# Second MLP layer, second token chunk: seven quarter products in place of sixteen plain units, for batches 2 to 7

## The chip, the cores and the metric

The kernel runs on one core of one Trainium2 chip. The time is the device time in microseconds (us) of one execution. TensorE is called PE below, VectorE DVE, ScalarE ACT, GpSimd POOL and the engine that issues the DMAs SP, as in the profile.

## The reference, cut to what matters

```python
# q, k, v: (8 batches, 8 heads, 576 tokens, 64), float32; w_ch1: (512, 2048); w_ch2: (2048, 512)
scores = q @ k.T / 8                              # per batch and head
scores = where(scores >= 32nd largest of its row, scores, -1e9)
x = (softmax(scores) @ v) -> (8, 576, 512)        # heads side by side
u = x + real(fft(fft(x, axis=1), axis=2))
un = (u - mean(u)) / sqrt(var(u) + 1e-6)          # over the 512 channels
out = u + relu(un @ w_ch1) @ w_ch2                # float32, (8, 576, 512)
```

## The kernel before

Batches are counted from 0 in the code (`b`); "batches 2 to 7" of the title are `b` = 1 to 6.

**One loop over attention tiles sets the order.** `items` holds 288 tiles of 128 query rows and one head (36 in a batch). Each turn of the last loop is a step: it issues, by hand and in a fixed order, the scores of a tile to come (PE, line 360, copied out by ACT in line 363), the search for the 32 largest values of a tile (DVE, lines 381 and 383: four `max`, three `match_replace`), the mask (ACT, line 397, then a subtraction on POOL, line 400), the exponential (ACT, line 406), the transposes (PE, line 427, copied out by ACT in line 430) and, at the end of a head pair, the product with v (PE, line 464). Every engine runs what it is given strictly in that order, and waits where an operand is not there.

**The rest of a batch is fitted into these steps.** When the four head pairs of batch b are done, its Fourier transform follows while the tiles of batch b+1 run: folded sums on POOL (lines 549, 565, 602), two pairs of transforms over the tokens (`dft_tokens`, line 634, PSUM tiles `yp_{b}_{par}_0` and `_1`; ACT copies each of them out with three instructions, lines 658 to 660), then the transforms over the channels (`dft_channels`, line 682, tiles `mp`; ACT copies `us` out, line 699; POOL adds them, line 705), the transposes of the normalised rows (line 747, tiles `tpu`), and then the MLP as a queue of units.

**The MLP units.** `mlp_units(b)` makes a list: for chunk 0 (tokens in tiles 0, 1 and the 64 rows of tile 4: 320 columns) and chunk 1 (tiles 2 and 3: 256 columns) 16 units `hidden` (four matmuls each, line 832, ReLU by ACT in line 836 into `hT`), and then the second layer. `one_unit` takes the next of the queue; `level` spreads the queue over the steps up to the next batch's arrival, so that PE gets about the same planned time in each step. `dft_tokens` first takes all `hidden` units that are still in the queue.

**The second layer in its two forms.** The plain form, `back` (line 859), has for each tile of 128 tokens 8 units of two matmuls of 512 columns; the sum stays in one PSUM bank, is scaled by ACT into a buffer (line 886; `hT`'s spare end for tile 2) and added to x by POOL (line 888), and for tile 3 it is scaled and added by DVE in one instruction (line 874). The form in seven products, `fast` (line 1029 for all its matmuls), takes the two tiles and the two halves of the hidden dimension as a 2 by 2 matrix of quarters and does with 7 products of quarters what takes 8: 14 units `p2 p1 p5 p4 p6 p3 p7`, each in two parts, of four matmuls of 256 columns. For that

- POOL forms sums of quarters of `hT` in place (`mix`, line 974, four of them in two parts each: quarters "21", "11", "12", "22"),
- SP brings sums of quarters of `w2`, kept in DRAM, into the places of two quarters of `w2` (`bring`, line 775: T1 and T2 into `w2_12`, T4 and T3 into `w2_21`, then the originals B12 and B21 again),
- five results go through ACT (line 999, into `room(n)`) and POOL (line 1001) into x, and two by DVE (line 987).

`later` puts POOL's part on a list `sums`, from which `some_sums` takes what fits into a step; `need` forces an entry out just before the PE instruction that depends on it. Two PSUM tiles are held through the seven products: `cv` (p2, p5, p3) and `cw` (p1, p4, p6, p7).

**The three banks.** `hidden`, `back`, `fast`, `yp`, `mp` and `tpu` (for all but the last batch, whose `yp`, `mp` and `tpu` have other banks) share three PSUM banks, handed out by `bank`: it takes the first of the list `banks_free` and, unless the tile is held, puts it at the end again at once. A held tile takes its bank off the list until it is freed.

In the kernel before, the seven products are used for chunk 0 of every batch but the first, and for both chunks of the last batch; chunk 1 of `b` = 1 to 6 and all of `b` = 0 use `back`.

Of the kernel before, what the change touches and what calls it, by code (L numbers as in the profile page):

```python
# [64 lines left out]
def kernel(  # L65
# [20 lines left out]
    NIT = DF // P  # L86
# [7 lines left out]
    CW = (2 * P + TAIL, 2 * P)  # L94
# [26 lines left out]
    def bank(shape, name, hold=False):  # L121
        n = banks_free.pop(0)
        t = ps_m.tile(shape, F32, name=name, tag=f"m{n}", bufs=1)
        if not hold:
            banks_free.append(n)
            return t
        return t, lambda: banks_free.append(n)
# [638 lines left out]
    DH = DM // 2  # L766
# [5 lines left out]
    def bring(o, place, part):  # L772
        kcs = slice(NK // 2 * part, NK // 2 * (part + 1))
        dst = place[part] if isinstance(place, list) else place[:, kcs]
        nc.sync.dma_start(out=dst, in_=scr[:, o, kcs, :])
# [19 lines left out]
    sums, summed = [], set()  # L795
# [8 lines left out]
    def need(key):  # L804
        if key in summed:
            return

        kind = next(s[3] for s in sums if s[0] == key)
        for s in [s for s in sums if s[3] == kind]:
            sums.remove(s)  # L810
            s[2]()
            summed.add(s[0])
            if s[0] == key:
                break
# [3 lines left out]
    def mlp_units(b):  # L818
        x = x_of[b]
        last = b == B - 1  # L820
        hTs, hT_of = {}, {}

        def hidden(ch, it):
            w, unT = CW[ch], unT_of[b, ch]
            if ch not in hTs:
                hTs[ch] = batp.tile([P, NIT, CW[0]], F32, name=f"hT_{b}_{ch}", tag="hT")
                hT_of[ch] = hTs[ch].rearrange("p i c -> p (i c)")[:, 0:NIT * w].rearrange(
                    "p (i c) -> p i c", c=w
                )
            hp = bank([P, CW[0]], f"hp_{b}_{ch}_{it}")  # L830
            for dt in range(NDT):
                nc.tensor.matmul(  # L832
                    hp[:, 0:w], lhsT=w1[:, dt, P * it:P * (it + 1)], rhs=unT[:, dt, 0:w],
                    start=(dt == 0), stop=(dt == NDT - 1),
                )
            nc.scalar.activation(out=hT_of[ch][:, it, :], in_=hp[:, 0:w], func=AF.Relu)  # L836
# [10 lines left out]
        def ct_tile():  # L847
            if not cts:
                cts.append(batp.tile([P, 3, DM], F32, name=f"ct_{b}", tag="fold_s"))
            return cts[0]  # L850
# [83 lines left out]
        def fast(ch):  # L934
# [22 lines left out]
                }  # L957

            def room(n):
                return ct_tile().rearrange("p t c -> p (t c)")[:, DH * n:DH * (n + 1)]  # L960

            def later(key, us, fn, soon=False):

                n = sum(s[3] for s in sums) if soon else len(sums)
                sums.insert(n, ((b, ch, *key), us, fn, soon))
                if last:
                    need((b, ch, *key))
# [12 lines left out]
            def to_x(t, cols, src, n, then=lambda: None):  # L980


                xt = x[:, t, cols].rearrange("p (e c) -> p e c", c=DH)
                e = xt.shape[1]
                if n is None or last:
                    def add():
                        nc.vector.scalar_tensor_tensor(
                            out=xt,
                            in0=src.rearrange("p (e c) -> p e c", e=1).to_broadcast([P, e, DH]),
                            scalar=rs[:, t:t + 1], in1=xt, op0=ALU.mult, op1=ALU.add,  # L990
                        )
                        then()
                    if last:
                        add()
                    else:
                        late_next.append(add)
                    return
                r = room(n)
                nc.scalar.mul(out=r, in_=src, mul=rs[:, t:t + 1])
                xt = x[:, t, cols]  # L1000
                later(("x", n), 0.75, lambda: nc.gpsimd.tensor_tensor(
                    out=xt, in0=xt, in1=r, op=ALU.add
                ))
# [20 lines left out]
            def product(name, cols, a, rhs_of, part, start):  # L1024


                dst = half_bank(name, cols)
                for kc in range(NK // 2 * part, NK // 2 * (part + 1)):
                    nc.tensor.matmul(  # L1029
                        dst, lhsT=h()[a][:, kc, :], rhs=rhs_of(kc), start=start and kc == 0,  # L1030
                        stop=kc == NK - 1, skip_group_check=True,
                    )
                return dst
# [10 lines left out]
            def p2(part):  # L1044
                c = product("v", lo, "12", lambda kc: w2_21[:, kc], part, True)
                if not last:
                    bring(T4, second, part)
                if part:
                    to_x(ta, lo, c, 0)

            def p1(part):
                c = product("w", lo, "11", b11, part, True)
                if part:
                    to_x(ta, lo, c, 1)
                    mix("11", "21", "11")
                    mix("12", "12", "11")

            def p5(part):
                need((b, ch, "21", part))
                c = product("v", hi, "21", first, part, False)  # L1060
                bring(T2, w2_12, part)
                if part:
                    to_x(tb, hi, c, 2)
# [9 lines left out]
            def p6(part):  # L1073
                need((b, ch, "11", part))
                c = product("w", lo, "11", first, part, False)
                if ch == 0:
                    bring(B12, w2_12, part)
                if part:
                    to_x(ta, hi, c, 4)
# [15 lines left out]
            def begin():  # L1095
# [7 lines left out]
            ] + [  # L1103
                (1.75, lambda f=f, part=part: f(part), "back")
                for f in (p2, p1, p5, p4, p6, p3, p7) for part in range(2)
            ]

        units = []
        for ch in range(2):
            units += [  # L1110
                (8 * CW[ch] / 1200.0, lambda ch=ch, it=it: hidden(ch, it), "hidden")
                for it in range(NIT)
            ]
            seven = b and ch == 0 or last
            if seven:
                begin, products = fast(ch)
                units.insert(1 - NIT, begin)
                units += products
            for t in [t for t in CHUNKS[ch] if t == 4 or not seven]:
                units += [  # L1120
                    (1.75, lambda ch=ch, t=t, p=p: back(ch, t, p), "back")
                    for p in range(4 if t == 4 else 8)
                ]
# [120 lines left out]
    for b in range(B):  # L1244
        end = PER_BATCH * (b + 1) - 1
        last = b == B - 1
# [45 lines left out]
        for n, t in enumerate((0, 1, 4, 2, 3)):  # L1292
            quick = first or last
            s = fc + (0 if first else n // 3 if last else n // 2)
# [7 lines left out]
        at(s + 1, "begin" if quick else "dve", lambda b=b: rsqrt(b))  # L1302
        arrivals.append(s + (1 if quick else 2))
        at(arrivals[-1], "units", lambda b=b: (queue if b else waiting).extend(mlp_units(b)))

    queue, waiting, pending, written, now, out_next = [], [], [], set(), [0], []
# [40 lines left out]
    i, carry = 0, 0.0  # L1347
# [157 lines left out]
```

## Time and profile before

| what | value |
|---|---|
| time, median of 4 runs (lowest, highest) | 1911.6 us (1910.61, 1913.67) |
| time of the profiled execution | 1910.46 us |
| its span, first to last instruction | 1908.7 us |
| mean granted PE clock | 0.974 |
| busy: PE, weight loads, DVE, ACT, POOL | 94%, 62%, 83%, 63%, 46% of the span |
| matmuls of the plain form, `cp` L859 | 512 records, 240.6 us busy |
| matmuls of the seven products, `cw` and `cv` L1029 in `w` | 448 and 384 records, 106.8 and 90.7 us busy |
| `mix` on POOL, L974 | 64, mean 1276 ns |
| DMA queue 1 | 109.33 MB, 20.2% of 16 engines |
| the chain that ended last | PE 79%, DVE 9%, ACT 6% |

How to read it: a float32 matmul of the program shows as two records, so two matmuls of 512 columns are "x4" in the timeline, and four of 256 columns "x8". The mean duration of a matmul overlaps with the next; what one costs is the distance from its start to the start of what follows. "Idle before" names what the engine waited for.

### The profile page before, as it was taken

The page shows a single profiled execution, that of the slowest core. Times are in us where ns is not written, and L with a number is a line of the kernel's source. Part 1 is how long each engine was busy: PE and PEld are TensorE (multiplying, and loading weights), DVE is VectorE, ACT ScalarE, POOL GpSimd, SP SyncE. Part 2 cuts the span into 40 slices and gives each one's busy share as a digit, 9 for nine tenths or more (in the row PEclk, how much of TensorE's full clock was granted, in tenths as well). Part 3 has the DMA queues.
Part 4 walks back from the last instruction along what each step waited for, and adds up shares of the span by engine and source line. Part 5 has one row for each costly group of instructions (what it writes and reads, how often), then busy time and mean ns, then how long its engine had stood idle before and what let it go on. Part 6 is the DMA issues. An engine that isn't in the chain of part 4 may idle for free.

```text
span 1908.7 us, 28279 instructions
## 1 busy us (share of the span) xinstructions
PE 1799.8 (94%) x9008; PEld 1192.5 (62%) x9008; DVE 1582.0 (83%) x3277; ACT 1210.3 (63%) x3078; POOL 876.5 (46%) x1158
## 2 busy tenths in 40 slices
PE   6567799999999999999999999999999999999999
PEld 3344465474666756766567656667567656667677
DVE  7999989999999999989898998888899898862110
ACT  6878657676766767666666667666676667652100
POOL 4768543545534454345535454345535454341012
PEclk7778899999999999999999999999999999999999
DMA  5323002211114111140014101140013102030132
GB/s 168 112 85 108 20 13 63 86 56 25 47 24 120 31 26 41 45 118 19 22 44 114 43 15 50 42 121 19 19 47 101 52 17 59 23 103 6 50 106 74
DMA packets 184340, 111.34 MB, mean 58 GB/s; under 512 B 125953, under 2 KB 174209, under 8 KB 184193
## 3 DMA queue, kind: packets, MB, share of 16 engines
q1 hardware_dynamic: 183408, 109.33, 20.2%
q8 instruction: 72, 1.18, 0.3%
q14 instruction: 76, 0.61, 0.1%
q10 hardware_dynamic: 784, 0.21, 0.1%
HBM read 93.76 MB, written 15.73 MB: 57 GB/s over the span
## 4 chain that ended last, share of the span: by engine, by line
PE 79%; DVE 9%; ACT 6%; POOL 2%; DMA 2%; issue 2%; SPq 0%; POOLq 0%; DVEq 0%; ACTq 0%
PE hp L832 25%; PE cp L859 11%; PE o L464 7%; PE tpP L427 6%; PE sp L360 6%; PE cw L1029 5%; PE cv L1029 4%; DVE m L381 4%; PE mp L682 3%; PE yp L634 3%; DVE wk L383 3%; PE cp L898 3%; PE sp_t L330 2%; ACT wk L406 1%; POOL wk L400 1%
## 5 line engine op out<-in xcount | busy, mean ns | idle before, releaser
L400 POOL TENSOR_TENSOR wk<-S,wk 128x576 f32<-128x576 f32 x288 | 408.5, 1418 | 775.0 <-ACT wk L397 745.9
L381 DVE MAX8 m<-wk 128x8 f32<-128x576 f32 x864 | 626.3, 749 | 6.1
L832 PE MATMUL hp<-unT,w 128*128 128x256 f32 (+1 forms) x2048 | 538.2, 409 | 2.6 <-ACT unT L750 2.6
L832 PEld LDWEIGHTS hp<-unT,w 128*128 128x128 f32 x2048 | 373.6, 191 | 124.1 <-issue 24.8
L383 DVE MATCH_REPLACE8 wk<-m,wk 128x576 f32<-128x576 f32 x576 | 427.5, 742 | 0.0
L406 ACT ACTIVATE wk<-wk,nt 128x576 f32<-128x576 f32 x288 | 224.8, 781 | 70.1 <-POOL wk L400 66.0
L427 PE MATMUL tpP<-ident,wk 128*128 128x128 f32 x1152 | 183.2, 283 | 67.5 <-ACT wk L406 43.7
L430 ACT COPY PT<-tpP 128x512 f32<-128x512 f32 (+1 forms) x320 | 171.3, 546 | 111.2 <-PE tpP L427 108.9
L859 PE MATMUL cp<-w,hT 128*128 128x512 f32 x512 | 240.6, 598 | 0.0
L397 ACT ACTIVATE wk<-S,nt 128x576 f32<-128x576 f32 x288 | 226.9, 788 | 17.2 <-POOL nt L390 16.0
L427 PEld LDWEIGHTS tpP<-ident,wk 128*128 128x128 f32 x1152 | 140.7, 145 | 141.3 <-ACT wk L406 64.8
L836 ACT ACTIVATE hT<-hp 128x320 f32<-128x320 f32 (+1 forms) x256 | 104.9, 410 | 193.8 <-PE hp L832 191.7
L381 DVE MAX8 m<-S 128x8 f32<-128x576 f32 x288 | 213.7, 742 | 5.3 <-ACT S L334 5.3
L383 DVE MATCH_REPLACE8 wk<-m,S 128x576 f32<-128x576 f32 x288 | 213.6, 742 | 0.0
L464 PE MATMUL o<-PT,v 128*64 128x256 f32 (+3 forms) x1440 | 193.3, 411 | 2.0 <-ACT PT L430 1.9
L363 ACT COPY S<-sp 128x512 f32<-128x512 f32 (+1 forms) x264 | 141.9, 589 | 54.1 <-PE sp L360 53.9
L360 PE MATMUL sp<-kT,qT 64*128 64x512 f32 (+1 forms) x528 | 161.2, 669 | 4.2 <-ACT means L1217 3.3
L464 PEld LDWEIGHTS o<-PT,v 128*64 128x64 f32 x1440 | 110.7, 151 | 72.8 <-issue 15.7
L859 PEld LDWEIGHTS cp<-w,hT 128*128 128x128 f32 x512 | 88.8, 190 | 86.3 <-issue 86.2
L974 POOL TENSOR_TENSOR hT<-hT 128x512 f32<-128x512 f32 x64 | 81.5, 1276 | 100.8 <-ACT hT L836 89.1
L1029 PE MATMUL cw<-w,hT 128*128 128x256 f32 x448 | 106.8, 383 | 2.3 <-POOL nt L390 1.2
L1029 PEld LDWEIGHTS cw<-w,hT 128*128 128x128 f32 x448 | 81.4, 190 | 20.0 <-issue 5.2
(143 smaller groups left out, 2149.0 us busy)
## 6 DMA issues: line engine op xcount, KB each, us to landing
w<-w_parts SPq DMA_DIRECT2D x82, 512.0 KB, 4.4
space<-in_moe_w_ch_dram SPq DMA_DIRECT2D x32, 512.0 KB, 3.5
nat<-in_q_dram SPq DMA_DIRECT2D x128, 64.0 KB, 2.1
v<-in_v_dram SPq DMA_DIRECT2D x128, 64.0 KB, 2.1
out_dram<-x SPq DMA_DIRECT2D x32, 256.0 KB, 2.1
nat<-in_k_dram SPq DMA_DIRECT2D x124, 64.0 KB, 2.1
w_parts<-w_t SPq DMA_DIRECT2D x8, 512.0 KB, 2.9
w_s<-w_parts SPq DMA_DIRECT2D x8, 512.0 KB, 5.0
```

Of the source, the lines that this page charges most:

```text
L360: nc.tensor.matmul(sp[r], lhsT=qT[hd, q_cols], rhs=kT[hd, :], start=True, stop=True)
L381: ops.append(lambda src=src, m8=m8: nc.vector.max(out=m8, in_=src))
L383: ops.append(lambda src=src, m8=m8: nc.vector.match_replace(w, m8, src, NEG))
L397: nc.scalar.activation(out=w, in_=Ssb[i], func=AF.Relu, scale=-FAR, bias=Nt[i][:, 1:2])
L400: nc.gpsimd.tensor_tensor(out=w, in0=Ssb.pop(i), in1=w, op=ALU.subtract)
L406: nc.scalar.activation(out=w, in_=w, func=AF.Exp, bias=Nt.pop(i)[:, 0:1], accum_out=den_t[pair % 3][:, c:c + 1],)
L427: nc.tensor.transpose(tp[:, c, :], p_sb[:, k0 + P * c:k0 + P * (c + 1)], ident)
L430: nc.scalar.copy(out=pt[:, NF * he:NF * (he + 1), col:col + w], in_=tp[:, :, o:o + w])
L464: nc.tensor.matmul(o[D * e:D * (e + 1), c0:c1], lhsT=vv[:, c, e, :], rhs=pt[:, 2 * NF if c == NF else NF * e + c, c0:c1], start=(c == 0), ...
L832: nc.tensor.matmul(hp[:, 0:w], lhsT=w1[:, dt, P * it:P * (it + 1)], rhs=unT[:, dt, 0:w], start=(dt == 0), stop=(dt == NDT - 1),)
L859: nc.tensor.matmul(cp, lhsT=hT[:, it, P * n:P * (n + 1)], rhs=w2[:, it, :], start=(it == 0), stop=(it == NIT - 1),)
L1029: nc.tensor.matmul(dst, lhsT=h()[a][:, kc, :], rhs=rhs_of(kc), start=start and kc == 0, stop=kc == NK - 1, skip_group_check=True,)
```

## The change

Chunk 1 of batches `b` = 1 to 6 is put through `fast` as well (`seven = b > 0`). The results of its five scaled products go into the four places of 256 columns that `hT`'s buffer has left over behind chunk 1's 16 x 256 columns; the fifth takes the first place again, after its POOL addition has been issued. Where a new `hT` tile is begun, all entries that are still on the list `sums` are issued first. B12 is brought back after p6 in these chunks too.

```diff
         def hidden(ch, it):
             w, unT = CW[ch], unT_of[b, ch]
             if ch not in hTs:
+                for s in list(sums):
+                    need(s[0])
                 hTs[ch] = batp.tile([P, NIT, CW[0]], F32, name=f"hT_{b}_{ch}", tag="hT")
...
             def room(n):
+                if ch:
+                    n0 = NIT * CW[1] + DH * (n % 4)
+                    return hTs[1].rearrange("p i c -> p (i c)")[:, n0:n0 + DH]
                 return ct_tile().rearrange("p t c -> p (t c)")[:, DH * n:DH * (n + 1)]
...
+                if ch and n == 4:
+                    need((b, ch, "x", 0))
                 r = room(n)
                 nc.scalar.mul(out=r, in_=src, mul=rs[:, t:t + 1])
...
                 c = product("w", lo, "11", first, part, False)
-                if ch == 0:
+                if not (last and ch):
                     bring(B12, w2_12, part)
...
-            seven = b and ch == 0 or last
+            seven = b > 0
```

## Prediction

> **What bounds the kernel now.** I read the busy times by window first. A middle batch lasts 216.23 us, from one batch's first token transform to the next one's:
>
> ```profile
> core 0: us, PE busy (x) PEld busy (x) DVE busy (x) ACT busy (x) POOL busy (x), PEclk, DMA share, GB/s
> 891.89:1108.12 216.23, 215.08 (x1106) 142.87 (x1105) 192.22 (x398) 145.11 (x372) 99.16 (x137) 1.00 0.19 52
> ```
>
> PE has 1.15 us without work, DVE 24, POOL 117, and the clock is full. So in a middle batch, what PE is spared shortens the kernel, and what PE waits lengthens it. The PE timeline gives the price of a unit in both forms:
>
> ```profile
> 1022.52 1.89 PE L1029 MATMUL cw<-w,hT 128*128 128x256 f32 x8
> 1024.25 0.38 PE L504 MATMUL tpx<-ident,xT 128*128 128x128 f32 x2
> ...
> 1112.93 1.88 PE L859 MATMUL cp<-w,hT 128*128 128x512 f32 x4
> 1114.65 0.71 PE L274 MATMUL tpq<-ident,nat 128*128 128x128 f32 x5
> ```
>
> From start to next start, a unit of the seven products takes 1.73 us and a plain unit 1.72 us.
>
> **What it spares.** Chunk 1 has 16 plain units (27.5 us) and gets 14 (24.2 us): 3.3 us in each of six batches, **19.8 us**. In the order that the changed program issues, one unit less stands before the first token transform and one less after the second; thirteen stand between the two transforms in both. The weights are loaded 112 times instead of 64, 190 ns each; these loads run beside the matmuls, and the 1.73 us above already holds eight of them (1.52 us), so they cost nothing. Were they not hidden, 48 more would cost 9.1 us a batch. The Trainium skill ("Perfetto Trace Analysis", Identifying the Most-Contended Engine) wants TensorE judged by the busy share of the weight loads, not of the matmuls; by that the change would load the engine more, 55 us in all, and the row above decides against it.
>
> **What it costs: banks.** Two held tiles leave one of the three banks. In the order of bank uses before, no tile follows another at once in the same bank. In the changed program it happens at ten places where PE can go on only after ACT has copied the first tile out (a further six have other work between, or wait for the same copies anyway). The rows from before, with two banks to take turns, for PE and then ACT:
>
> ```profile
> 1147.30 0.41 PE L634 MATMUL yp<-fs,ftail 128*1 128x145 f32 x2
> 1147.65 0.76 PE L634 MATMUL yp<-fs,fg 128*128 128x145 f32 x4
> ...
> 1150.93 3.72 PE L682 MATMUL mp<-fd,y 128*128 128x256 f32 x16
> ```
>
> ```profile
> 1147.75 0.42 ACT L658 COPY y<-yp 128x288 f32<-128x288 f32 x1 [2.80 <-PE yp L634]
> 1148.06 0.30 ACT L659 COPY y<-yp 128x144 f32<-128x144 f32 x1
> 1148.22 0.41 ACT L660 ACTIVATE y<-yp,sg 128x144 f32<-128x144 f32 x1
> ...
> 1153.69 0.65 ACT L699 COPY us<-mp 128x512 f32<-128x512 f32 x1
> ```
>
> The second `yp` began at 1147.65, while ACT was still to copy the first until 1148.63. In one bank it begins 0.1 us after that: 1.1 us later. This is so in both pairs of b = 1 and in the second pair of b = 2 to 5: six times, **6.5 us**. In b = 2 and 5 p3 ends just before the second transform, so its bank is still held at the channel transforms, and the first two `mp` share one: the second would begin at 1152.65 (half of the group of 3.72), but the copy of the first ends at 1154.34, as ACT has masks and scores in front of it: 1.8 us, twice, **3.6 us**. At the start of the last batch the second `hp` waits for one ReLU (436 ns and the hand-over): **0.6 us**. The skill says it as a rule ("Perfetto Trace Analysis", Matmuls): "Independent matmul groups should rotate through different PSUM banks so the ACT/DVE evacuation of one overlaps the next group's matmuls". It sets no price; without these stalls the sum would be 10.7 us lower.
>
> **What it costs: POOL's sums.** Eight `mix` of 1276 ns and five additions of 730 ns replace one addition of 1272 ns: 12.6 us more POOL work a batch, now beside the folds. POOL has 117 us free, so the amount is hidden. What counts is the place in its queue. In this stretch the folds take what a step leaves for sums, so half of the mixes are forced out by `need`, behind that step's mask (L400). The rows of chunk 0 show how long that is, PE, ACT and POOL in turn:
>
> ```profile
> 1028.56 1.13 PE L360 MATMUL sp<-kT,qT 64*128 64x512 f32 x4
> 1029.62 1.99 PE L1029 MATMUL cw<-w,hT 128*128 128x256 f32 x8
> ...
> 1033.62 0.38 PE L330 MATMUL sp_t<-kt,qT 128*128 128x128 f32 x2
> 1034.39 1.97 PE L1029 MATMUL cw<-w,hT 128*128 128x256 f32 x8 [0.39 <-POOL nt L390]
> ```
>
> ```profile
> 1033.82 0.47 ACT L999 ACTIVATE ct<-cw,gi 128x256 f32<-128x256 f32 x1
> ```
>
> ```profile
> 1031.60 1.41 POOL L400 TENSOR_TENSOR wk<-S,wk 128x576 f32<-128x576 f32 x1 [3.79 <-ACT wk L397]
> 1032.97 1.28 POOL L974 TENSOR_TENSOR hT<-hT 128x512 f32<-128x512 f32 x1
> ```
>
> The scores of the step end at 1029.62; copies and the mask's ACT half follow, the mask starts at 1031.60 and the mix behind it ends at 1034.25: with the hand-over, 4.7 us after the scores. In the changed order PE reaches a product that needs such a mix after 2.16 us in b = 1 (p7) and b = 4 (p3; one unit and a transpose after the scores), after 3.9 in b = 3, and after about 4.65 in b = 2 and 5. Waits: 2.6 + 2.6 + 0.9 + 0.1 + 0.1 = **6.3 us**. In b = 6 no masks are left, and its mixes are early. Bounds: 0, if the mixes find POOL free earlier, and 13, if five batches wait 2.6 each.
>
> **What it costs: the shared result tile.** p6 adds to the bank whose other half ACT copies after p4. Above: p4 ends at about 1033.62, its copy at 1034.29, p6 starts at 1034.39, which is 0.77 later with 0.22 us of other work between (the profile puts it down to POOL's bounds, which were done; the copy fits to 0.1 us). In chunk 1 p6 follows p4 directly in b = 2 and 5 (0.7 each), with 0.54 us between in b = 3 and 4 (0.35 together); chunk 0 gets closer in b = 1 and 2 (0.5, 0.3). Together **2.5 us**, between 1 and 5, since the copy may also stand behind an exponential (781 ns).
>
> **The rest.** ACT gets 1.7 us more a batch (five copies of 474 ns for one of 687), DVE 0.5; both have over 20 us free, but a copy ahead of an exponential can hold a transpose up: 0 to 0.5 a batch, I take 0.2, **1.2 us**. DMA: twelve brings of 512 KB in each of six batches, 38 MB more to 111; SP issues one in 0.37 us. The closest use of a brought part lies about 9.7 us behind the product that frees its place, and a bring lands in 4.4 us (at most 6.8): hidden; if the cover were gone, a product would wait what is missing. The loads of q, k and v queued behind them on SP are used some 20 us later. The additions forced out at a new `hT` are five of 0.73 us on POOL, early in the hidden units: nothing waits for them. The last store of a batch, and with it the next use of x, moves by about a step, for which `xT` has room.
>
> **The sum.** −19.8 + 10.7 + 6.3 + 2.5 + 1.2 = +0.9 us on 1910.46, which is 1911.4; the median lies 1.1 above the profiled execution: **1912.5 us**. About 0.2% (3.8 us) can be told from no change here: between 1907.8 and 1915.4 I call it the same.
>
> **Rivals.**
> - *The stalls are smaller* (chance 0.22). If PE's waits for POOL and for p4's copy overlap with others, or mixes come early (their lower bounds: 0 and 1), the sum is −19.8 + 10.7 + 1 + 0 = −8.1: about 1903.5. For it: in the chunk 0 products of the middle batch PE waited 0.39 us in all. Against: the folds, which chunk 0 does not meet.
> - *Slower: the mixes set PE's pace between the transforms* (0.36). Place: p3 and p7 behind a mask's sum on POOL. Price: 2.6 us in each of five batches, 13 instead of 6.3, and p4's copy at 5: 1921.7 at most, about 1919 half-way. It decides once PE gets to these products less than 4.7 us after a step's scores. For it: POOL waits 109.8 us of a batch's 216 for the masks of ACT, and each such wait now also holds the mix behind it. Against: in three of five batches there is nearly enough work between.
> - *DVE takes over*: 192.7 us of 216 leaves 23; no chance given by itself.
>
> **How the numbers follow.** The forecast, within 0.2%, has 0.42. The range from 1905 to 1920 takes in the first rival's nearer half and the second up to its middle price; its ends are the bounds of the POOL and copy terms.
>
> **What would show it.** In the profile after: L1029 records up by 672, L859 down by 384; PE idle before `yp` with ACT `y` named, about 1 us, six times; about 1.8 us before `mp` in two batches; waits of `cv` and `cw` for POOL `hT` of 2 to 3 us in two batches; the batch period nearly 216 us. I am wrong if PE's waits in a middle batch stay under 2 us (then it is 8 us or more faster), or if new waits appear that none of these names: for DMA `w`, or for ACT's exponentials.

## The result, and the profile after

The changed kernel takes 1914.6 us (median of 37 runs, 1911.7 to 1917.3) against 1911.7 (55 runs, 1909.4 to 1914.6). The ratio is 1.0015, its 95% interval 1.0011 to 1.0020: 2.9 us longer, inside the 3.8 us that the prediction calls the same, 2.1 us above its 1912.5. The profiled execution took 1915.24 us, its span 1913.4.

4.7 us lie between the two spans, but 1.9 of them come before the first token transform (at 235.13 us, before at 233.27), where both kernels issue the same instructions; over all the traces below this stretch took 232.5 to 235.2 us. The change answers for the remaining 2.85. The busy times by window, after, for three middle batches (before, the same three took 216.23 to 216.30 us, with PE busy for 215.08 to 215.15):

```profile
core 0: us, PE busy (x) PEld busy (x) DVE busy (x) ACT busy (x) POOL busy (x), PEclk, DMA share, GB/s
893.97:1111.01 217.04, 212.66 (x1154) 151.94 (x1152) 193.12 (x399) 146.13 (x376) 110.99 (x149) 1.00 0.29 81
1111.01:1327.09 216.08, 213.00 (x1155) 152.31 (x1154) 194.79 (x405) 147.52 (x378) 110.98 (x149) 1.00 0.30 81
1327.09:1545.79 218.70, 214.09 (x1153) 153.13 (x1151) 190.47 (x395) 144.67 (x374) 111.23 (x149) 0.99 0.29 80
```

PE has 2.4 and 2.2 us less work in the first two, and 4.4 and 3.1 us of idle time where it had 1.15, so the period stays at 216 to 217. In the third the idle time is 4.6 us, and the mean clock is 0.99, not 1.00. POOL has the 12 us more that were expected, and DVE is within 3 us of before. What the idle time is, in the waits of PE over the whole execution (us in total, times, longest; the changed program's lines are 1036 for the products, 979 for `mix`, 834 and 838 for the hidden units and their ReLU; L390 is where POOL forms `nt`, the bounds of the rows' masks):

```profile
PE yp L634 <- ACT y L660: 5.8, 6, 1.0
...
PE cv L1036 <- POOL hT L979: 3.1, 3, 2.2
...
PE mp L682 <- ACT us L699: 2.9, 2, 1.4
...
PE cw L1036 <- issue: 2.2, 3, 1.4
...
PE cw L1036 <- POOL nt L390: 2.0, 4, 0.6
...
PE cw L1036 <- POOL hT L979: 1.8, 1, 1.8
...
PE hp L834 <- ACT hT L838: 0.6, 1, 0.6
```

Before, `cw` waited 1.4 us under the names POOL `nt` and issue; the other five lines are new. All seven are kinds of wait that the prediction names; "issue" and POOL `nt` are the names that the profile gives to the wait of p6 for ACT's copy, as experiments 7 and 8 show. The groups of the page show that the work itself is as announced, 672 records of the seven products more (448 + 384 before) and 384 of the plain form less (512 before):

```profile
L1036 PE MATMUL cw<-w,hT 128*128 128x256 f32 x832 | 197.7, 382 | 6.9 <-issue 2.2 <-POOL nt L390 2.0 <-POOL hT L979 1.8
...
L1036 PE MATMUL cv<-w,hT 128*128 128x256 f32 x672 | 161.1, 385 | 3.1 <-POOL hT L979 3.1
...
L861 PE MATMUL cp<-w,hT 128*128 128x512 f32 x128 | 61.0, 600 | 0.0
```

The timeline shows what the first and the third line of the waits are made of, here where b = 2's chunk 1 meets the transforms of batch 3; first the second `yp`, then the second `mp`:

```profile
932.88 0.41 ACT L658 COPY y<-yp 128x288 f32<-128x288 f32 x1 [2.65 <-PE yp L634]
933.18 0.29 ACT L659 COPY y<-yp 128x144 f32<-128x144 f32 x1
933.35 0.40 ACT L660 ACTIVATE y<-yp,sg 128x144 f32<-128x144 f32 x1
...
933.81 0.76 PE L634 MATMUL yp<-fs,fg 128*128 128x145 f32 x4 [0.96 <-ACT y L660]
...
939.85 0.64 ACT L699 COPY us<-mp 128x512 f32<-128x512 f32 x1
...
940.54 1.99 PE L682 MATMUL mp<-fd,y 128*128 128x256 f32 x8 [1.45 <-ACT us L699]
```

Each starts 0.05 to 0.06 us after the last copy out of the bank that it shares with its predecessor. And the second line of the waits, at its longest, p3 of b = 4:

```profile
1359.88 0.60 PE L427 MATMUL tpP<-ident,wk 128*128 128x128 f32 x4
...
1360.03 1.41 POOL L400 TENSOR_TENSOR wk<-S,wk 128x576 f32<-128x576 f32 x1 [3.61 <-ACT wk L397]
...
1361.40 2.49 POOL L979 TENSOR_TENSOR hT<-hT 128x512 f32<-128x512 f32 x2
...
1362.72 3.68 PE L1036 MATMUL cv<-w,hT 128*128 128x256 f32 x8 [2.23 <-POOL hT L979]
...
1366.23 0.39 PE L330 MATMUL sp_t<-kt,qT 128*128 128x128 f32 x2
```

The mix stands behind the mask, and the mask had let POOL wait 3.61 us. But look at the product itself: eight records from 1362.72 to 1366.23, 3.5 us instead of 1.73. Windows of 3.41 us around it, the length of the pieces in which the clock is recorded, show why:

```profile
1359.40:1362.81 3.41, 1.18 (x8) 0.81 (x7) 2.00 (x4) 2.01 (x4) 2.78 (x3) 1.00 0.36 124
1362.81:1366.22 3.41, 3.41 (x8) 2.71 (x9) 0.00 (x0) 0.00 (x0) 2.44 (x3) 0.50 0.00 0
1366.22:1369.64 3.42, 3.42 (x24) 3.20 (x23) 2.53 (x5) 1.77 (x6) 1.91 (x2) 1.00 0.00 0
```

PE was busy for 1.18 us of the first, and got half its clock in the second. That was in no step of the prediction. It does not come with every such wait: the traces of experiments 1, 2 and 8 (the changed kernel alone) have the same one of 2.2 us, and no half clock behind it.

**The account of PE** after the first token transform, from the starts of its records (what passes from a start to the next start, less listed idle time, belongs to the operation): 384 records of plain units gone, -168.8 us; 672 records of the seven products more, +149.1 at full clock, so -19.7 together; half clock +1.7 (another such stretch, near 253 us, is in both kernels); listed waits +17.2 (24.4 to 41.6); everything else +3.7, in hand-overs and waits under 0.15 us, which no view lists; 1.8 of it lies in the matmuls of the hidden units, the rest in small amounts on most operations, and its cause is open. The sum is +2.9, the 2.85 from above. The account compares one execution of each kernel.

### The profile page after: what moved, and what is told of

Same layout as the page of the kernel before. It is cut to its first block, busy times and chain, and to the rows that moved or that the text cites. A ratio compares the mean times of both kernels' runs of the same rounds, so it can differ in the third digit from the quotient of the medians.

```text
span 1913.4 us, 29046 instructions
## 1 busy us (share of the span) xinstructions
PE 1783.1 (93%) x9296; PEld 1245.3 (65%) x9296; DVE 1591.1 (83%) x3283; ACT 1215.4 (64%) x3102; POOL 949.8 (50%) x1230
## 4 chain that ended last, share of the span: by engine, by line
PE 78%; ACT 7%; DVE 7%; POOL 4%; issue 2%; DMA 2%; SPq 0%; POOLq 0%; ACTq 0%; DVEq 0%
PE hp L834 25%; PE cw L1036 9%; PE o L464 8%; PE cv L1036 7%; PE sp L360 6%; PE tpP L427 6%; PE mp L682 4%; PE yp L634 3%; DVE m L381 3%; PE cp L900 3%; DVE wk L383 2%; POOL wk L400 2%; PE cp L861 2%; PE sp_t L330 2%; ACT wk L406 1%
## 5 line engine op out<-in xcount | busy, mean ns | idle before, releaser
L427 PE MATMUL tpP<-ident,wk 128*128 128x128 f32 x1152 | 182.7, 283 | 69.2 <-ACT wk L406 41.6
L1036 PE MATMUL cw<-w,hT 128*128 128x256 f32 x832 | 197.7, 382 | 6.9 <-issue 2.2
L979 POOL TENSOR_TENSOR hT<-hT 128x512 f32<-128x512 f32 x112 | 144.2, 1291 | 115.8 <-ACT hT L838 95.5
L1036 PEld LDWEIGHTS cw<-w,hT 128*128 128x128 f32 x832 | 151.6, 190 | 36.4 <-issue 9.8
L1036 PE MATMUL cv<-w,hT 128*128 128x256 f32 x672 | 161.1, 385 | 3.1 <-POOL hT L979 3.1
L1036 PEld LDWEIGHTS cv<-w,hT 128*128 128x128 f32 x672 | 123.4, 192 | 28.5 <-issue 7.2
```

The costliest lines, as they stand in the source:

```text
L427: nc.tensor.transpose(tp[:, c, :], p_sb[:, k0 + P * c:k0 + P * (c + 1)], ident)
L979: nc.gpsimd.tensor_tensor(out=v[dst][:, k], in0=v[a][:, k], in1=v[c][:, k], op=op)
L1036: nc.tensor.matmul(dst, lhsT=h()[a][:, kc, :], rhs=rhs_of(kc), start=start and kc == 0, stop=kc == NK - 1, skip_group_check=True,)
```

## The experiments

Ratios are to the kernel before, run on the same chip beside each (1910.4 to 1911.0 us); the changed kernel stands at 1.0015. The theory: PE is the bound and the named waits, one by one, are what ate the gain. The rival: each wait only stands in for another, or another engine takes over.

**1. Banks of the transposes.** In `half_of_tokens` and `dft_channels`:

```diff
-        yp = ps_t.tile(shape, F32, name=name, tag="tp") if b == B - 1 else bank(shape, name)
+        yp = ps_t.tile(shape, F32, name=name, tag="tp") if b == B - 1 or b and g2 else bank(shape, name)
...
-        mp = ps_s.tile(shape, F32, name=name, tag="sp") if b == B - 1 else bank(shape, name)
+        mp = (ps_s.tile(shape, F32, name=name, tag="sp") if b == B - 1 else
+              ps_t.tile(shape, F32, name=name, tag="tp") if b and t in (1, 2) else bank(shape, name))
```

> The change, with the second yp of each pair and every second mp of the batches b = 1 to 6 in the banks of the attention's transposes (tag tp) instead of the three of bank(). Theory A (PE is the bound and the new waits for a bank are what ate the gain): PE's waits before yp (5.8 us in the trace of the changed kernel) and before mp (2.9) go, and the time falls by all of it, 8.7 us, from 1914.6 to about 1906. Rival B (the wait only moves): PE waits as long before the transposes tpP, whose two banks are now shared, or for ACT elsewhere: 1912 to 1915.

Measured 1912.06 us, ratio 1.0011 (1.0002 to 1.0020). The rival held: the lines of `yp` <- `y` and of `mp` are gone from PE's waits, and there are new ones:

```profile
PE tpP_t L438 <- ACT y L660: 5.3, 10, 0.5
...
PE tpP_t L442 <- ACT us L700: 1.4, 5, 0.3
...
PE yp L634 <- ACT qT L282: 1.1, 1, 1.1
```

The transposes' two banks are used again within 0.43 us of PE work, so the wait moved to the next user.

**2. Banks of the scores.** The same two tiles in the other pool:

```diff
+        yp = (ps_t.tile(shape, F32, name=name, tag="tp") if b == B - 1 else
+              ps_s.tile(shape, F32, name=name, tag="sp") if b and g2 else bank(shape, name))
...
+        mp = ps_s.tile(shape, F32, name=name, tag="sp") if b == B - 1 or b and t in (1, 2) else bank(shape, name)
```

> The change, with the second yp of each pair and every second mp of b = 1 to 6 in the two banks of the scores (tag sp) instead of the three of bank(). The first try, with the banks of the transposes, only moved the waits: tpP_t follows a yp or mp there after 0.43 us. In the scores' banks the next user comes at least 1.4 us of PE work later in b = 2 to 6. Theory A (the waits for a bank cost what they last, since PE is the bound): 5.8 + 2.9 us before yp and mp go and nothing comes in their place: 8.7 us less than the changed kernel, ratio to before about 0.997. Rival B: PE stands instead before the scores sp: ratio 1.0005 or more.

1903.81 us, ratio 0.9966 (0.9954 to 0.9979): 9.4 us under the changed kernel, where 8.7 were expected. The waits of `yp` and `mp` for ACT are gone and none came for them; the scores' own records took 2.4 us longer. So the agreement with 8.7 is in part luck: in the traces the listed waits fell by 9.5 us and 1.7 us of half clock did not occur, and 2.4 us came back on the scores. With experiment 1 it shows that another bank alone does not help; the work between two uses of it is what differs, 0.43 us there and at least 1.4 here in b = 2 to 6.

**3. The control: the same edit without the change.**

> A control: the kernel before (plain form for chunk 1) with only the edit of the banks: the second yp of each pair and every second mp of b = 1 to 6 in the banks of the scores. Theory A (the edit pays only where the change made one bank out of three serve everything): PE waited for no bank before yp or mp in the kernel before, so nothing can go: ratio 0.999 to 1.001. Rival B (the edit is worth something by itself, so that its gain says nothing on the change): ratio 0.997 or less, as with the change.

1912.72 us, ratio 1.0012 (1.0003 to 1.0020). Nothing to gain where nothing waited, and the 2.5 us on the scores' records are there too. So the 9.4 us of experiment 2 are a cost of the change.

**4. All mixes ahead of the folds.** At the end of a step:

```diff
+        for s in [s for s in sums if s[3]]:
+            need(s[0])
         run(i, "pool0")
```

> The change, with all sums of quarters (mix) that are due put ahead of the folds on POOL at the end of each step, so that none waits for a step's mask. Theory A: PE's waits of cv and cw for POOL hT (4.9 us) go, and with the longest of them the 3.4 us of half clock that follow it (1.7 us): 6.6 us less than the changed kernel, about 1908. Rival B (POOL's queue is what counts): up to four mixes of 1.28 us in a row hold up the next mask, the exponential and the transposes behind it: PE waits for ACT wk instead, 1914 to 1920.

1927.65 us, ratio 1.0090 (1.0076 to 1.0104): the rival, and worse than it said. Its timeline at b = 5, POOL, ACT and PE:

```profile
1566.94 4.97 POOL L979 TENSOR_TENSOR hT<-hT 128x512 f32<-128x512 f32 x4
...
1571.86 2.51 POOL L565 TENSOR_TENSOR zw<-sd 128x512 f32<-128x512 f32 x2
...
1575.41 1.40 POOL L400 TENSOR_TENSOR wk<-S,wk 128x576 f32<-128x576 f32 x1 [0.20 <-ACT wk L397]
...
1577.77 0.66 PE L427 MATMUL tpP<-ident,wk 128*128 128x128 f32 x4 [1.29 <-ACT wk L406]
...
1580.85 0.78 ACT L406 ACTIVATE wk<-wk,nt 128x576 f32<-128x576 f32 x1 [0.88 <-POOL wk L400]
...
1581.62 0.45 ACT L1006 ACTIVATE hT<-cw,gi 128x256 f32<-128x256 f32 x1
1582.18 3.17 PE L1036 MATMUL cw<-w,hT 128*128 128x256 f32 x8 [1.91 <-issue]
```

Four mixes and two folds fill 7.5 us of POOL; the mask comes without its usual idle time before it, which means late; the transposes wait for its exponential, and ACT's copy of p4 stands behind an exponential that is late as well, so that p6 waits 1.91 us. After the first token transform the transposes' waits for the exponential come to 13.7 us, where they are 8.5 in the changed kernel, and three stretches of 3.41 us after 300 us run at half clock; the p6 above, 3.17 us long, lies in one of them. POOL was idle for half of the batch, and yet there was no room in this step. With the banks of experiment 1 it came to the same, more strongly:

> Both edits, of the banks and of the mixes. Theory A (PE waits add up, since PE is the bound): 8.7 + 6.6 = 15.3 us less than the changed kernel, about 1899, 0.6% under the kernel before. Rival B (another engine takes over once PE is relieved, DVE or the chain of masks): no lower than about 1907.

1932.1 us, ratio 1.0114 (1.0100 to 1.0128): theory A was wrong by 33 us, and the rival's bound holds for another reason than DVE or the masks alone. Its clock shows five stretches of 3.41 us at 0.5 after 300 us, where the changed kernel has one; the waits that the new banks bring (5.3 and 1.4 us, as in experiment 1) are there as well.

**5. Two mixes a step, where they are.** Behind folds and bounds:

```diff
-        some_sums(1.3)
+        some_sums(2.6 if sums and sums[0][3] and sums[0][0][1] else 1.3)
```

> The change, with two sums of quarters (mix) instead of one let through on POOL at the end of a step, behind the folds and the bounds, when they are of chunk 1. None is then left to be forced out behind the mask that PE waits for; at most two stand in a row, where the first try put four ahead of the folds. Theory A: the 4.9 us of cv and cw waiting for POOL hT go, and the half clock after the longest (1.7 us): 6.6 us less than the changed kernel, ratio to before 0.998. Rival B (every mix between two masks delays the next exponential, wherever it stands): PE waits for wk in tpP, ratio 1.0015 or more.

1908.05 us, ratio 0.9987 (0.9978 to 0.9996): 5.4 us less, of 6.6 expected. No wait for `hT` on POOL is left, and no stretch at half clock after 300 us. But one line has come, at two p6 that had waited 0.61 us each before, under the name of POOL's bounds (`nt`):

```profile
PE cw L1036 <- POOL fg L549: 3.1, 2, 1.6
```

**6. Scores' banks and two mixes.**

> Both: yp and mp in the banks of the scores, and two mixes a step. Theory A (PE waits add up): 15.3 us less than the changed kernel, ratio to before about 0.9935, close to the 0.9932 of the kernel with 14 plain units. Rival B: what one edit frees the other or the masks take back, ratio 0.998 or more.

1900.86 us, ratio 0.9951 (0.9938 to 0.9965): 12.2 us under the changed kernel, of 15.3. Of the missing 3.1, 1.9 stand in the line above, which this kernel has as well (3.1, 2, 1.6). The 2.3 us on the scores' records of experiment 2 are there too, and in the profiled execution a stretch at half clock at 477.60 us, behind a wait of 2.28 us before a transpose. The profile names a fold on POOL, but no product reads one. In its timeline at b = 2, PE's p4, then ACT, then PE's p6:

```profile
914.79 1.89 PE L1037 MATMUL cw<-w,hT 128*128 128x256 f32 x8
...
916.91 0.78 ACT L406 ACTIVATE wk<-wk,nt 128x576 f32<-128x576 f32 x1 [1.27 <-POOL wk L400]
...
917.68 0.46 ACT L1007 ACTIVATE hT<-cw,gi 128x256 f32<-128x256 f32 x1
...
918.24 1.97 PE L1037 MATMUL cw<-w,hT 128*128 128x256 f32 x8 [1.56 <-POOL fg L549]
```

p6 starts 0.1 us after ACT's copy of p4 out of the same bank, and that copy waited behind an exponential, and the exponential for POOL's mask. This was tested by taking the two apart:

**7. The last products woven.** On top of 6, with the mixes of 11 and 12 issued in turn by parts:

```diff
-                for f in (p2, p1, p5, p4, p6, p3, p7) for part in range(2)
+                for f, part in [(f, n) for f in (p2, p1, p5, p4) for n in range(2)]
+                + [(p3, 0), (p6, 0), (p6, 1), (p3, 1), (p7, 0), (p7, 1)]
```

> Scores' banks and two mixes a step, and the last products in another order of parts: p3a p6a p6b p3b p7a p7b instead of p6a p6b p3a p3b p7a p7b, with the mixes of 11 and 12 in turn by parts, in both chunks. A part of p3 then lies between p4 and p6, which PE started late behind ACT's copy of p4 (in the run before, with scores' banks and two mixes: 1.45 us once, 1.56 twice, 0.39 six times). Theory A (that copy is what PE waited for, though the profile names POOL there): these 6 to 7 us go, ratio to before about 0.992. Rival B (it was POOL, as the profile says, or p3 now comes ahead of its mix): PE waits as long before cv, ratio 0.995 or more.

1892.0 us, ratio 0.9905 (0.9890 to 0.9920). All waits of `cw` and `cv` are gone from the list, so it was the copy and not POOL: p3's first part now stands where p6 stood, its sum comes behind p6's on POOL, which works in order, and it does not wait. Two middle batches:

```profile
887.43:1100.70 213.27, 212.30 (x1154) 152.30 (x1152) 192.99 (x400) 145.91 (x376) 111.06 (x149) 1.00 0.30 82
1100.70:1314.54 213.84, 212.67 (x1154) 152.55 (x1153) 194.84 (x405) 147.55 (x378) 110.97 (x149) 1.00 0.29 82
```

PE is idle for about 1 us of each again, as before the change, with 2.5 to 2.8 us less work. This version beats both kernels, by 18 us and 21 us.

**8. Two controls for the order.** The woven order in the kernel before:

> A control: the kernel before with the woven order of parts (p3a p6a p6b p3b p7a p7b) in the seven products that it has, chunk 0. Theory A (the gain of the order is in what the change puts close together): before, PE waits at these places for 0.39 us in three batches, so no more than 1.5 us can go: ratio 0.999 to 1.000. Rival B (the woven order is worth as much without the change): ratio 0.996 or less.

1907.35 us, ratio 0.9983 (0.9974 to 0.9992). That is 3.2 us, more than theory A allowed: in the trace the listed waits fell by 2.3 us and the records of `cw`, `sp_t` and others by 1.4. So of the 18 us of experiment 7 some 3 have nothing to do with the change; with the order alike on both sides, the change with all three edits is worth 0.9905/0.9983 = 0.9922, 15 us. And in the changed kernel alone:

> The change with the woven order alone, banks and mixes as the change has them. Theory A (three separate waits, each for itself): p6's wait for ACT's copy goes (2.8 us), the waits for banks stay (9 us), and p3a, now one product earlier, waits more often for its mix, which is still let through one a step: 0 to 1.7 us more in each of five batches. Ratio to before 1.000 to 1.004. Rival B (the order alone is what frees PE, and the other two edits add little): ratio 0.996 or less.

1904.14 us, ratio 0.9967 (0.9954 to 0.9980), and theory A was wrong: 9.2 us less. The waits for banks (5.8 and 2.9) and for mixes (3.1 and 1.8) are the same as in the changed kernel to 0.1 us, so p3's first part did not come too early for its mix. All lines of `cw` for copies, 4.2 us, are gone; waits under 0.15 us fell by some 3; and the 1.7 us of half clock did not occur, though the wait of 2.23 us did. The rival is not shown either: its 0.996 was not reached, and the other two edits add 12 us to this one (experiment 7). One by one the three edits are worth 9.4, 5.4 and 9.2 us, 24.0 in all, and together 21.0: the waits add up nearly, as the theory has it.

**9. The saving by itself.** The kernel before, 14 plain units in place of 16:

```diff
-                    for p in range(4 if t == 4 else 8)
+                    for p in range(4 if t == 4 else 8) if not (ch and 0 < b and not last and p == 6)
```

> The kernel before (plain form for chunk 1) with the seventh of the eight units of tiles 2 and 3 left out in b = 1 to 6: 14 units in place of 16 and no other change, so the part of the product over hidden columns 1536 to 1791 is missing there. It measures what 12 units less are worth on PE. Theory A (PE bound, unit of 1.72 to 1.76 us to the next start): 20.6 to 21.1 us less than before, about 1891. Rival B (half or more of the gain is lost to other engines already here, without any new wait): 1900 or more.

1897.43 us, ratio 0.9932 (0.9919 to 0.9944): 13.3 us, not 21, between what the theory and the rival allowed. The missing units are 21.2 us in the trace, as computed. Against them stand 4.8 us of new listed waits (among them 1.45 us of a p6 of chunk 0, the same that the changed kernel has, and 1.95 before a transpose at 1416 us) and some 2 us in other records. `level` lays out the steps anew for a shorter queue; that some steps then no longer have their waits covered is a reading that no run tests. Part of the loss thus needs no seven products.

**10. The clock.** Two more operations on POOL ahead of p3, in chunk 1 of b = 1 to 6:

```diff
+                if ch and not last and part == 0:
+                    v, u = h()["12"][:, 0:NK // 2], h()["21"][:, 0:NK // 2]
+                    for op in (ALU.add, ALU.subtract):
+                        nc.gpsimd.tensor_tensor(out=v, in0=v, in1=u, op=op)
```

> The change, with two more sums (an addition and its undoing, about 2.55 us on POOL) right ahead of p3 in chunk 1 of b = 1 to 6: a longer wait of PE at a known place, six times. Theory A (PE idle for more than about half of a 3.41 us stretch halves its clock in the next one): the waits of cv for POOL grow by 2 to 2.5 us each, 12 to 15 us in all, and behind most of them stands a stretch of 3.41 us at clock 0.5 that costs another 1.7 us: about 1935 us, with four or more such stretches in the clock after 300 us. Rival B (the one half-clock stretch at 1363 us was chance): no more than one such stretch and 1927 to 1930 us.

1948.37 us in its one execution. The waits grew by as much as theory A had or more (2.5 us in b = 1, 3.1 to 3.7 in b = 2 to 5, 6.5 in b = 6), and in all six batches the clock fell to half, for 34 us in all. In b = 2 to 6 it fell behind a stretch that the wait of p3 had left with 0.00 to 1.51 us of PE work. In b = 1 it did not: that wait of 2.84 us fell across two stretches and left PE busy for 2.44 and 1.56 us of them, and the half clock came behind p7's wait of 2.22 us for its own sum, with PE busy for 1.19 us. The waits, and the stretch of b = 3 with the one after it:

```profile
PE cv L1036 <- POOL hT L1093: 26.0, 6, 6.5
```

```profile
1152.17:1155.58 3.41, 0.03 (x1) 0.00 (x0) 2.67 (x5) 1.52 (x4) 3.33 (x3) 1.00 0.58 175
1155.58:1158.99 3.41, 3.21 (x8) 2.59 (x9) 0.00 (x0) 0.00 (x0) 3.41 (x5) 0.50 0.03 9
```

## Why the prediction was right, and where it was not

The time, the sign within the error and the reason hold: PE is spared 20 us of products and made to wait for about as much. By the steps of the sum, predicted and measured:

| term | predicted | measured |
|---|---|---|
| 96 plain units for 84 of the products | -19.8 | -19.7 |
| six `yp` in one bank | 6.5 | 5.8 |
| two `mp` in one bank | 3.6 | 2.9 |
| `hp` of the last batch | 0.6 | 0.6 |
| products behind a mask's mix | 6.3 | 4.9 |
| p6 behind the copy of p4 | 2.5 | 2.9 |
| ACT ahead of transposes | 1.2 | 0.1 at most |
| half clock after a wait | none | 1.7 |
| hand-overs and short waits | none | 3.7 |
| sum | +0.9 | +2.9 |

- **The saving.** Its price by start-to-start distances was right: over the whole trace a plain unit cost 1.76 us and one of the products 1.78, 0.04 to 0.05 more than the rows used, which cancels. The weight loads (now 65% of the span, 62 before) were hidden, as the timeline said. The Trainium skill ("Perfetto Trace Analysis", Identifying the Most-Contended Engine) names two measures for TensorE, MFU (operations done as a share of what its peak rate would do) and the busy share of the weight loads; the prediction mentions only the second, which alone would have shown more load, but in experiment 7 as many loads go with 18 us less time.
- **The banks.** All nine places of the sum were right (the prediction's text says ten, its terms and the trace have nine), `hp` to the tenth and the others a bit dear: 0.96 to 1.01 us where 1.1 was taken, 1.45 where 1.8 was. The rule of the Trainium skill ("Perfetto Trace Analysis", Matmuls) that was set beside them holds here, and experiments 2 and 3 give it a price: 9.4 us gained by taking turns, where tiles followed each other in one bank, and nothing gained (2.3 us lost) where they did not.
- **POOL.** Right by place: 1.81 for p7 of b = 1 and 2.23 for p3 of b = 4 (2.6 each predicted), 0.51 in b = 3 (0.9), none in b = 2 and 5 (0.1 each), and 0.36 at b = 1's p3, not predicted. The 4.7 us from the scores to the product, taken from a row of chunk 0, came out as 4.7 in b = 1, 3 and 4 too. What was too small is the work that PE has in the meantime: 2.4 to 2.5 us in b = 1 and 4 (2.16 taken) and 4.16 in b = 3 (3.9).
- **p6.** Right in size, wrong in place: half of it is the 1.45 us in chunk 0 of b = 1, where 0.5 was taken; there the copy (591.80 to 592.27 us) stands behind 1.5 us of ACT's copies of scores and 0.77 of a mask, and p6 starts at 592.38. The two of 0.7 in chunk 1 measured 0.61 each, and the 0.35 of b = 3 and 4 did not come.
- **What was not seen.** The costs were put 3.5 us too high, and 5.4 us were left out: the half clock, and the hand-overs and short waits. These two errors cancel for the most part; that the forecast is so near is in part luck.
- **The rivals.** That stalls are smaller did not come true in this kernel, but experiments 2, 5 and 7 show what it would have been worth. That mixes set the pace is what experiments 4 and 10 show, at 1928 and 1948 us, once a few more POOL operations are in the wrong place. DVE did not take over: its 190 to 195 us stayed below PE's 212 in every batch shown, those of experiment 7 included. The numbers around the rivals are loose in the prediction: the first one's sum leaves out the 1.2 us of "the rest" (with it 1904.7), and the range's ends, 1905 and 1920, are not quite the bounds of the terms (1904.7 and 1921.7).

## What to carry to other kernels

When an engine is the bound, count what a change spares it, and then walk through the order in which it will meet its buffers: for each tile, which one had the buffer before, how much of its own work lies between, and how long the copy-out takes. Here that told nine stalls of 0.6 to 1.5 us in advance. The same walk also tells which other bank is free long enough (1.4 us of work) and which is not (0.43), but here the second was seen only after experiment 1 had moved the waits. A half-idle engine in strict order has room only between its own deadlines: two sums behind the folds gained 5 us on the changed kernel, four ahead of them lost 14.

## What the runs showed of the hardware that was not expected

**Short waits can halve TensorE's clock.** The clock is granted in stretches of 3.41 us. Cutting the 14 traces at those bounds after the first token transform gives some 6,800 stretches at full clock: the 24 in which PE was busy for 1.51 us or less were all followed by one at half clock, of the ten between 1.54 and 1.61 us six were, and of all others one (2.19 us). Fourteen of these 31 are one and the same early place, 251 to 254 us, which every trace has, so they are fewer cases than they look; the other 16 of the 24 lie in five traces. So a wait of about 2 us was enough where it fell into one stretch. Where it fell across two, the clock stayed full: the same wait of 2.24 us in experiment 2, over the bound at 1355.57:

```profile
1352.15:1355.57 3.42, 2.83 (x16) 1.94 (x12) 3.39 (x9) 2.30 (x4) 1.03 (x1) 1.00 0.72 229
1355.57:1358.98 3.41, 1.76 (x8) 1.58 (x9) 0.36 (x1) 0.91 (x3) 3.41 (x5) 1.00 0.02 6
1358.98:1362.39 3.41, 3.41 (x24) 3.18 (x23) 2.53 (x5) 1.77 (x6) 2.63 (x3) 1.00 0.00 0
```

The price is 1.7 us for each such stretch that is full of work. The Trainium skill ("TensorE: Matmul & The Clock Gate", What's actually happening) gives the same length, free-running, and has the clock fall after an idle window of it; here a window in which PE was busy for up to 1.51 us of 3.41 was enough, and the measurement decides.

**The name behind a wait can be wrong.** Waits put down to POOL's fold, to POOL's bounds and to "issue" were all ACT's copy out of a shared bank: woven apart, they went together, 4.2 us in experiment 8 and 6.1 in experiment 7. Start of the waiting instruction minus end of each candidate (0.1 us for the copy) told it before the run did.
